# Issue order from estimated engine clocks, score bursts of three, and one shared set of PSUM banks in an attention and feed-forward kernel

## The chip, the cores and the metric

One core of a Trainium2 chip. The metric is the device time of one execution in microseconds (us); a *span* is the time from the first to the last instruction of the execution that was profiled. The kernel before takes 388.7 us (median of 3 runs, 388.52 to 390.5). The experiments ran in three batches, each on another chip (6, 8 and 13 in the record), and each batch timed the kernel before again, so a ratio compares runs of one batch. All runs told of here were in the fast state. The engines are called PE (TensorE), ACT (ScalarE), DVE (VectorE), POOL (GpSimd) and SP (SyncE, which issues most transfers).

## The reference

Attention with normalised queries and keys over 8 batches of 12 heads, 448 positions, 64 wide; then a feed-forward part over all 3584 positions.

```python
q_n, k_n = rmsnorm(q, g_q), rmsnorm(k, g_k)           # over the 64
scores = scale * np.matmul(q_n, k_n.transpose(0, 1, 3, 2))
attn = softmax(scores)                                # over the keys
x = np.matmul(attn, v)            # -> (3584, 768), heads side by side
a, b = x @ w1, x @ w2             # (768, 1024) each
h = a * b @ w3                    # (1024, 1024)
out = h @ w_out                   # (1024, 768), float32
```

Both kernels multiply w3 by w_out once (the matmuls called wps), so that the last two products are one.

## The kernel before

The kernel treats four heads at a time, 24 such sets. A set is 7 *score units*; a unit is 8 matmuls (sc) into two banks of PSUM, the memory that matmuls write to, and one exponential on ACT (P, or Pr for the last unit of a set). Three *pv* sets follow: one sums the exponentials (its logarithm and exponential, r, come from ACT), two give x (DVE multiplies by r into xT). Three sets of heads make a batch; then come its 8 pairs of pa (x times w1, copied to a_sb) and pb (x times w2, multiplied by a_sb into abT) and its po groups (copied to o_sb and stored). While PE has no work at the start, it runs matmuls whose results nobody reads (warm). All this is laid out in slots of two score units by tables:

```python
    sc_psum = ctx.enter_context(tc.tile_pool(name="sc_ps", bufs=2, space=PSUM))   # 2 x 2 banks
    mm_psum = ctx.enter_context(tc.tile_pool(name="mm_ps", bufs=4, space=PSUM))   # 4 x 1 bank
    ffn_pool = ctx.enter_context(tc.tile_pool(name="ffn", bufs=2))     # a_sb
    out_pool = ctx.enter_context(tc.tile_pool(name="outp", bufs=2))    # o_sb
    # ... tables: which slot has which part of the preparation, how many wps ...

    def qk_exp(n):
        # ...
        sc = sc_psum.tile([NP, 2, 512], FP, tag="sc", name="sc")
        for c0 in range(0, NP, 32):
            # ...
            for u in range(2):
                nc.tensor.matmul(
                    out=sc[c0 : c0 + 32, u, 0:S],
                    lhsT=qkT[u * D : (u + 1) * D, pr, 1, k0 : k0 + 32],
                    rhs=qkT[u * D : (u + 1) * D, pr, 0, 0:S],
                    start=True, stop=True, tile_position=(u * D, c0),
                )
        # ...
        nc.scalar.activation(out=dst, in_=sc[:, :, 0:S], func=AF.Exp)

    # a_sb is always copied by ACT, o_sb always by DVE:
        nc.scalar.copy(out=a_sb, in_=ps[:, 0:S])
        nc.vector.tensor_copy(out=o_sb[:, nh * NH : (nh + 1) * NH], in_=ps[:, 0:NH])

        for t in range(max(todo) + 1):
            # ... loads of this slot
            for n in range(2 * t, min(2 * t + 2, NQ * NU)):
                qk_exp(n)
            # ...
            for i, kind in todo.get(t, []):
                pv_set(i, kind)
            # ... weight loads, wps, or so many pa/pb/po from the list
            # ... preparation (square, reduce, scale, transpose) of later heads
```

Of the kernel before, what the change touches and what calls it, by code (L numbers as in the profile page):

```python
# [18 lines left out]
def kernel(  # L19
# [31 lines left out]

    const = ctx.enter_context(tc.tile_pool(name="const", bufs=1))
# [6 lines left out]
    ffn_pool = ctx.enter_context(tc.tile_pool(name="ffn", bufs=2))  # L59
    out_pool = ctx.enter_context(tc.tile_pool(name="outp", bufs=2))  # L60
    sc_psum = ctx.enter_context(tc.tile_pool(name="sc_ps", bufs=2, space=PSUM))
    mm_psum = ctx.enter_context(tc.tile_pool(name="mm_ps", bufs=4, space=PSUM))
# [3 lines left out]
    N_PE_T = 5  # L66
    N_SQ_ACT = 24
    W34_EV = 'DA'
    W34_NARROW = False
    WARM = (16, 2, 11, 3, 5, 0)  # L70
    LAG = 8
    UNITS = 3.0
    V_COST = 0.4
    V_AHEAD = 2
    MOVE = 2
    LOADS_0 = ['w0', 'w3', 'w1', 'o0', 'w2']
    LOADS_1 = ['w4', 'v0', 'w7', 'w6', 'w5', 'v1', 'o1', 'v2']
    GATE = ('q', 2)
    QK1_AT = 0
    SHIFT = [0, -1, -1, -1, -3, -3, -3]  # L80
    PREP_1 = {'sq0': -3, 'red0': -6, 'sq1': -6, 'red1': -3, 'alpha': -8, 'sc0': -3, 't0': -2, 'sc1': -2, 't1': 0}
    PREP = {'load': -7, 'sq0': -5, 'red0': -5, 'sq1': -4, 'red1': -4, 'alpha': -3, 'sc0': -3, 't0': -1, 'sc1': -2, 't1': -1}
    W34_SLOTS = {1: 2, 2: 1, 3: 2, 4: 3, 5: 1, 6: 1, 7: 3, 8: 1, 9: 1, 10: 2, 11: 2, 12: 3, 13: 2}
# [18 lines left out]

    qk_bufs = [
# [6 lines left out]
    halves = ((0, REST, J, 0, SPLIT), (REST, NP, NF, SPLIT, S))  # L110

# [6 lines left out]
    def load_qk(i, split=1, k_eng=None):  # L118
        b, m = divmod(i, NQB)
        s = st[i]  # L120
        s["q"], s["k"] = qk_bufs[i % 3]
        n = HQ // split
        for h0 in range(0, HQ, n):
            for t_sb, src, eng in (
                (s["q"], q, nc.sync),
                (s["k"], k, k_eng or nc.sync),
            ):
                for p0, p1, nj, t0, t1 in halves:
                    eng.dma_start(  # L129
                        out=t_sb[p0:p1, h0 : h0 + n, 0:nj, :].rearrange(  # L130
                            "p h j d -> p h (j d)"
                        ),
                        in_=src[b, HQ * m + h0 : HQ * m + h0 + n, t0:t1].rearrange(
                            "h (p j) d -> p h (j d)", j=nj
                        ),
                    )
# [57 lines left out]
    def prep_sq(i, pr, on_act=False):  # L194
        s = st[i]
        if pr == 0:
            s["ssq"] = prep_pool.tile([NP, 2, HQ, J], FP, tag="ssq", name="ssq")
        sq = prep_pool.tile([NP, 2, 2, J, D], FP, tag="sq", name="sq")
        s["sq", pr] = sq
        hs = slice(2 * pr, 2 * pr + 2)  # L200
        for t, src in enumerate((s["q"], s["k"])):
            if on_act:
                nc.scalar.activation(out=sq[:, t], in_=src[:, hs], func=AF.Square)  # L203
            else:
                nc.gpsimd.tensor_tensor(
                    out=sq[:, t], in0=src[:, hs], in1=src[:, hs], op=MULT
                )

    def prep_red(i, pr):
        s = st[i]  # L210
        hs = slice(2 * pr, 2 * pr + 2)
        sq = s.pop(("sq", pr))
        for t in ((0, 1), (1, 2)) if i == 0 else ((0, 2),):
            nc.vector.tensor_reduce(  # L214
                out=s["ssq"][:, slice(*t), hs, :], in_=sq[:, slice(*t)], axis=AX, op=ADD
            )

    def prep_alpha(i, h0=0, h1=HQ):
        s = st[i]
        if h0 == 0:  # L220
            s["lnv"] = prep_pool.tile([NP, 2, HQ, J], FP, tag="lnv", name="lnv")
            s["alpha"] = prep_pool.tile([NP, 2, HQ, J], FP, tag="alpha", name="alpha")
        lnv = s["lnv"][:, :, h0:h1]
        nc.scalar.activation(out=lnv, in_=s["ssq"][:, :, h0:h1], func=AF.Ln, bias=eps_t)
        nc.scalar.activation(  # L225
            out=s["alpha"][:, :, h0:h1], in_=lnv, func=AF.Exp, scale=-0.5
        )

    def prep_scale(i, pr, pe=False):
        s = st[i]  # L230
        hs = slice(2 * pr, 2 * pr + 2)
        if pr == 0:
            s["qkT"] = qkT_pool.tile([128, 2, 2, J * NP], BF, tag="qkT", name="qkT")
        alpha = s["alpha"]
        qtmp = prep_pool.tile([NP, J, 2, D], BF, tag="qtmp", name="qtmp")
        nc.vector.tensor_tensor(  # L236
            out=qtmp.transpose([0, 2, 1, 3]),
            in0=s["q"][:, hs],
            in1=alpha[:, 0, hs].unsqueeze(3).broadcast_to([NP, 2, J, D]),
            op=MULT,  # L240
        )
        qks = prep_pool.tile([NP, 2, J, 2, D], BF, tag="qks", name="qks")
        nc.vector.tensor_tensor(
            out=qks[:, 0],
            in0=qtmp,
            in1=g_b.unsqueeze(1).unsqueeze(1).broadcast_to([NP, J, 2, D]),
            op=MULT,
        )
        nc.vector.tensor_tensor(  # L249
            out=qks[:, 1].transpose([0, 2, 1, 3]),  # L250
            in0=s["k"][:, hs],
            in1=alpha[:, 1, hs].unsqueeze(3).broadcast_to([NP, 2, J, D]),
            op=MULT,
        )
        if pe:
            s["qks", pr] = qks
        else:
            issued.add(("t", i, pr))
            nc.sync.dma_start_transpose(
                out=s["qkT"][:, pr].rearrange("d t (j p) -> d (t j) p", p=NP),  # L260
                in_=qks.rearrange("p t j h d -> p (t j h d)"),
            )

    def prep_pe_transpose(i, pr):
        s = st[i]
        issued.add(("t", i, pr))
        qks = s.pop(("qks", pr))
        ps = mm_psum.tile([128, 2, S], BF, tag="mm", name="qkT_ps")
        for t in range(2):
            for j in range(J):  # L270
                n = NP if j < NF else REST
                nc.tensor.transpose(  # L272
                    ps[:, t, j * NP : j * NP + n], qks[0:n, t, j], ident[0:n, 0:n]
                )
        nc.vector.tensor_copy(out=s["qkT"][:, pr, :, 0:S], in_=ps)  # L275
# [4 lines left out]
    def qk_exp(n):  # L280
        i, g = divmod(n, NU)
        s = st[i]
        if g == 0:
# [3 lines left out]
        sc = sc_psum.tile([NP, 2, 512], FP, tag="sc", name="sc")  # L287
# [21 lines left out]
        nc.scalar.activation(out=dst, in_=sc[:, :, 0:S], func=AF.Exp)  # L309


    def pv_set(i, kind):
        s = st[i]
        b, m = divmod(i, NQB)
        ps = mm_psum.tile([128, S], FP, tag="mm", name="pv")
        for j in range(J):
            for h in range(HQ):
# [11 lines left out]
                )  # L329
        if kind == 0:  # L330
            s["r"] = att_pool.tile([128, S], FP, tag="r", name="r")
            nc.scalar.activation(out=s["r"], in_=ps, func=AF.Ln)
            nc.scalar.activation(out=s["r"], in_=s["r"], func=AF.Exp, scale=-1.0)
            return
        if b not in xT:
            xT[b] = x_pool.tile([128, CM, S], BF, tag="xT", name="xT")
        nc.vector.tensor_tensor(  # L337
            out=xT[b][:, 2 * m + kind - 1, :], in0=ps, in1=s["r"], op=MULT
        )
        if kind == 2:  # L340
# [4 lines left out]

    def w34_evac(dst, src, kind):
        if W34_EV[kind] == "A":
            nc.scalar.copy(out=dst, in_=src)
        else:
            nc.vector.tensor_copy(out=dst, in_=src)  # L350
# [11 lines left out]

    def w3_transpose(fc):
        assert ("w3", fc) in issued
        ps = mm_psum.tile([128, CF, 128], BF, tag="mm", name="w3T_ps")
# [4 lines left out]
        w34_evac(w3T[:, :, fc * 128 : (fc + 1) * 128], ps, 0)  # L370

    def w34_unit(fc, nh):
        assert ("o", nh) in issued
        ps = mm_psum.tile([128, 512], FP, tag="mm", name="wps")
        for gc in range(CF):
            lhsT = w3T[:, gc, fc * 128 : (fc + 1) * 128]
            rhs = w_outs[:, gc, nh * NH : (nh + 1) * NH]
            if W34_NARROW:
                narrow(ps, NH, lhsT, rhs, gc == 0, gc == CF - 1)
            else:  # L380
                nc.tensor.matmul(  # L381
                    out=ps[:, 0:NH], lhsT=lhsT, rhs=rhs,
                    start=(gc == 0), stop=(gc == CF - 1),
                )
        w34_evac(w34s[:, fc, nh * NH : (nh + 1) * NH], ps[:, 0:NH], 1)
# [3 lines left out]
    def ffn1_a(b, fi):  # L389
        ps = mm_psum.tile([128, 512], FP, tag="mm", name="pa")  # L390
# [6 lines left out]
        nc.scalar.copy(out=a_sb, in_=ps[:, 0:S])  # L397
        a_tiles[b, fi] = a_sb

    def ffn1_b(b, fi):  # L400
# [3 lines left out]
        ps = mm_psum.tile([128, 512], FP, tag="mm", name="pb")  # L404
        for c in range(CM):
# [4 lines left out]
        nc.vector.tensor_tensor(  # L410
            out=abT[bp][:, fi, odd * S : (odd + 1) * S],
            in0=ps[:, 0:S],
            in1=a_tiles.pop((b, fi)),
            op=MULT,
# [4 lines left out]
    def ffn2(bp, t, nh):  # L419
# [3 lines left out]
        ps = mm_psum.tile([128, 512], FP, tag="mm", name="po")  # L423
# [238 lines left out]
```

## Time and profile before

The numbers come from the trace: starts of PE's groups of matmuls, and the distance from each to the next.

| part of the span, us | before |
|---|---|
| up to the first pa | 71.3 |
| work after it, at PE's pace | 291.0 |
| entering and leaving score bursts after it (69 x 0.228) | 15.7 |
| all other loss after it | 4.9 |
| last matmul to the end | 4.3 |
| span | 387.2 |

"At PE's pace" means 47.25 ns for a matmul of 448 columns in a 32-column strip (four run side by side), 40.6 ns for one of 384, and 23.6 ns for a score matmul (eight side by side). In the lines of a profile, 128*128, 128*32 and 64*32 are PE's *tiling modes*: the rows and columns of its array that one matmul takes. The table is a difference of starts, not of busy time: the ends of matmuls are modelled, so a late start can hide inside a busy PE. The lines behind it are shown in the prediction below.

### The profile page before, as it was taken

How to read it: one execution, taken by the hardware profiler on the slowest of the kernel's cores; microseconds unless marked ns; L12 is line 12 of the kernel's file. 1: busy time of each engine (PE TensorE's matmuls, PEld its weight loads, DVE VectorE, ACT ScalarE, POOL GpSimd, SP SyncE). 2: the span in 40 equal slices, each digit the busy share in tenths (PEclk: the TensorE clock that was granted, in tenths of full speed). 3: DMA queues.
4: the chain of work that ended last, by engine and by line, in shares of the span. 5: the costliest groups of instructions: out<-in, count | busy, mean ns of one | idle time of the engine just before them, and what ended most of it. 6: DMA issues, size and time to landing. Idle time of an engine off the chain costs nothing.

```text
span 387.2 us, 17022 instructions
## 1 busy us (share of the span) xinstructions
PE 372.7 (96%) x7669; PEld 192.1 (50%) x7670; DVE 242.5 (63%) x398; ACT 265.7 (69%) x443; POOL 75.5 (19%) x131
## 2 busy tenths in 40 slices
PE   7869999999999998999999999999999999999995
PEld 2335545444544454444545455445544554556563
DVE  5877855557758665776678568587676684234232
ACT  3578897778678883888697866786788856730210
POOL 2526546322022202202202202220222000000000
PEclk9969999999999999999999999999999999999998
DMA  6999999787989839849978879868898564004005
GB/s 176 220 239 231 234 232 169 114 108 160 153 163 178 161 68 232 192 68 154 228 139 157 124 171 197 149 146 158 173 175 152 65 153 86 3 3 125 2 19 149
DMA packets 92972, 56.42 MB, mean 146 GB/s; under 512 B 56932, under 2 KB 86884, under 8 KB 92900
## 3 DMA queue, kind: packets, MB, share of 16 engines
q1 hardware_dynamic: 70208, 42.35, 50.8%
q0 software_dynamic: 21952, 12.33, 23.9%
q8 instruction: 60, 0.98, 1.1%
q10 hardware_dynamic: 740, 0.66, 0.7%
q14 instruction: 12, 0.10, 0.1%
HBM read 46.66 MB, written 11.01 MB: 149 GB/s over the span
## 4 chain that ended last, share of the span: by engine, by line
PE 79%; DMA 10%; DVE 4%; ACT 3%; SPq 2%; issue 1%; POOL 1%; DVEq 0%; ACTq 0%; POOLq 0%
PE pa L354 17%; PE pb L354 17%; PE po L354 15%; PE pv L322 13%; PE sc L297 9%; PE wps L381 6%; DMA out_dram<-o_sb 5%; DMA w_outs<-in_moe_w_out_dram 4%; PE qkT_ps L272 1%; ACT P L309 1%; DVE o_sb L430 1%; DVE ssq L214 1%; SPq L129 1%; DMA q_sb<-in_q_dram 1%; PE w3T_ps L367 1%
## 5 line engine op out<-in xcount | busy, mean ns | idle before, releaser
L309 ACT ACTIVATE P<-sc 128x896 bf16<-128x896 f32 x144 | 125.1, 913 | 28.9 <-PE sc L297 28.8
L354 PE MATMUL pa<-xT,w1s 128*32 128x448 bf16 x1536 | 83.9, 353 | 1.1 <-DVE xT L337 1.1
L354 PE MATMUL pb<-xT,w2s 128*32 128x448 bf16 x1536 | 83.8, 352 | 0.0
L152 POOL DMA_DIRECT2D v_sb<-in_v_dram x72 | 43.7, 620 | 198.1 <-PE pv L322 174.5
L354 PE MATMUL po<-w34s,abT 128*32 128x384 bf16 x1792 | 77.5, 326 | 1.7 <-DVE o_sb L430 1.7
L410 DVE TENSOR_TENSOR abT<-pb,a_sb 128x448 bf16<-128x448 f32 x64 | 39.8, 622 | 60.1 <-PE pb L354 45.6
L214 DVE TENSOR_REDUCE ssq<-sq 128x16 f32<-128x1024 f32 (+1 forms) x50 | 58.2, 1168 | 12.2 <-ACT sq L203 12.2
L397 ACT CAST a_sb<-pa 128x448 bf16<-128x448 f32 x64 | 33.9, 530 | 43.4 <-PE pa L354 43.3
L354 PEld LDWEIGHTS <-abT 128*32 128x32 bf16 x1792 | 48.1, 97 | 28.5 <-issue 2.2
L354 PEld LDWEIGHTS <-w1s 128*32 128x32 bf16 x1536 | 40.4, 97 | 34.8 <-issue 5.4
L354 PEld LDWEIGHTS <-w2s 128*32 128x32 bf16 x1536 | 41.4, 97 | 31.3
L430 DVE COPY o_sb<-po 128x384 f32<-128x384 f32 x56 | 30.4, 555 | 39.3 <-PE po L354 20.9
L297 PE MATMUL sc<-qkT 64*32 64x448 bf16 x1344 | 48.9, 357 | 0.2 <-DVE qkT L275 0.2
L236 DVE TENSOR_TENSOR qtmp<-q_sb,alpha 128x512 bf16<-128x512 f32 x48 | 32.9, 684 | 12.8 <-ACT alpha L225 10.9
L322 PE MATMUL pv<-P,v_sb 128*32 128x448 bf16 x576 | 36.0, 356 | 0.0
L337 DVE TENSOR_TENSOR xT<-pv,r 128x448 bf16<-128x448 f32 x48 | 29.6, 616 | 5.2 <-PE pv L322 3.4
L249 DVE TENSOR_TENSOR qks<-k_sb,alpha 128x512 bf16<-128x512 f32 x48 | 32.9, 684 | 0.0
L203 ACT ACTIVATE sq<-q_sb 128x512 f32<-128x512 f32 x48 | 30.2, 630 | 0.0
L203 ACT ACTIVATE sq<-k_sb 128x512 f32<-128x512 f32 x48 | 29.9, 623 | 0.0
L322 PEld LDWEIGHTS <-v_sb 128*32 128x32 bf16 x768 | 16.2, 95 | 24.0 <-issue 15.5
L297 PEld LDWEIGHTS <-qkT 64*32 64x32 bf16 x1344 | 12.2, 89 | 28.8 <-issue 27.4
L381 PE MATMUL wps<-w_outs,w3T 128*128 128x384 bf16 x128 | 24.7, 345 | 1.1 <-DMA w_outs<-in_moe_w_out_dram 1.1
(46 smaller groups left out, 243.3 us busy)
## 6 DMA issues: line engine op xcount, KB each, us to landing
out_dram<-o_sb SPq DMA_DIRECT2D x54, 192.0 KB, 3.3
q_sb<-in_q_dram SPq DMA_DIRECT2D x23, 256.0 KB, 3.8
k_sb<-in_k_dram SPq DMA_DIRECT2D x23, 256.0 KB, 4.7
q_sb<-in_q_dram SPq DMA_DIRECT2D x23, 192.0 KB, 4.4
k_sb<-in_k_dram SPq DMA_DIRECT2D x23, 192.0 KB, 5.4
v_sb<-in_v_dram POOLq DMA_DIRECT2D x24, 96.0 KB, 4.2
w3s<-in_moe_w_dram POOLq DMA_DIRECT2D x8, 256.0 KB, 9.6
w_outs<-in_moe_w_out_dram POOLq DMA_DIRECT2D x4, 384.0 KB, 10.7
```

The costliest lines, as they stand in the source:

```text
L152: nc.gpsimd.dma_start(out=dst.rearrange("p h j d -> p h (j d)"), in_=part.rearrange("p h j d -> p h (j d)"),)
L203: nc.scalar.activation(out=sq[:, t], in_=src[:, hs], func=AF.Square)
L214: nc.vector.tensor_reduce(out=s["ssq"][:, slice(*t), hs, :], in_=sq[:, slice(*t)], axis=AX, op=ADD)
L236: nc.vector.tensor_tensor(out=qtmp.transpose([0, 2, 1, 3]), in0=s["q"][:, hs], in1=alpha[:, 0, hs].unsqueeze(3).broadcast_to([NP, 2, J, D] ...
L297: nc.tensor.matmul(out=sc[c0 : c0 + 32, u, 0:S], lhsT=qkT[u * D : (u + 1) * D, pr, 1, k0 : k0 + 32], rhs=qkT[u * D : (u + 1) * D, pr, 0, 0:S],
L309: nc.scalar.activation(out=dst, in_=sc[:, :, 0:S], func=AF.Exp)
L322: nc.tensor.matmul(out=ps[h * HALF : (h + 1) * HALF, :], lhsT=w, rhs=s["P"][:, h, j, :] if j < NF else s["Pr"][:, h % 2, :], start=(j == 0 ...
L354: nc.tensor.matmul(out=ps[32 * h : 32 * h + 32, 0:n], lhsT=lhsT[:, 32 * h : 32 * h + 32], rhs=rhs, start=start, stop=stop, tile_position=( ...
L381: nc.tensor.matmul(out=ps[:, 0:NH], lhsT=lhsT, rhs=rhs, start=(gc == 0), stop=(gc == CF - 1),)
L397: nc.scalar.copy(out=a_sb, in_=ps[:, 0:S])
L410: nc.vector.tensor_tensor(out=abT[bp][:, fi, odd * S : (odd + 1) * S], in0=ps[:, 0:S], in1=a_tiles.pop((b, fi)), op=MULT,)
L430: nc.vector.tensor_copy(out=o_sb[:, nh * NH : (nh + 1) * NH], in_=ps[:, 0:NH])
```

## The change

Its intent is to let a model of each engine's clock, kept while the program is built, decide what is issued next, instead of tables. At the start the model also picks PE's next work. After that PE's order is still laid out by score unit (a pv set stands KIND units behind the last burst of its heads, and pa, pb and po are spread over what is left); the model then chooses the banks, the engine of each copy, and what ACT and DVE do in between. Scores come three units at a time. Any of the eight PSUM banks may serve any stage, the one that is estimated to be free first. A copy out of PSUM goes to the engine that is estimated to end it first. Weight loads are all queued at the start, behind a *gate*: a small copy on POOL that waits for a first transfer of queries. The queries of the first batch lie on 112 partitions, four rows each, so that one transfer brings them.

```diff
-    ffn_pool = ctx.enter_context(tc.tile_pool(name="ffn", bufs=2))
-    out_pool = ctx.enter_context(tc.tile_pool(name="outp", bufs=2))
-    sc_psum = ctx.enter_context(tc.tile_pool(name="sc_ps", bufs=2, space=PSUM))
-    mm_psum = ctx.enter_context(tc.tile_pool(name="mm_ps", bufs=4, space=PSUM))
+    G = 3
+    KIND = (3, 4, 6)
+    ffn_pool = ctx.enter_context(tc.tile_pool(name="ffn", bufs=F_BUFS))      # 3
+    out_pool = ctx.enter_context(tc.tile_pool(name="outp", bufs=O_BUFS))     # 3
+    ps_pool = ctx.enter_context(tc.tile_pool(name="ps", bufs=1, space=PSUM))
+    banks = ps_pool.tile([128, 8, 512], FP, name="banks_ps")
+    clk = {"PE": 0.0, "ACT": 0.0, "DVE": 0.0}
+    free = [0.0] * 8
+    def take(n):
+        z = min(range(9 - n), key=lambda a: (max(free[a : a + n]), a % n, a))
+        # ...
+    def evac(z, ready, engs, costs, fn):
+        ends = [max(clk[e], ready) + c + (BIAS if k else 0) for k, (e, c) in enumerate(zip(engs, costs))]
+        k = ends.index(min(ends))
+        # ... other work of ACT and DVE that fits before is issued first
+        fn(e)
# ... prep_red, prep_alpha and prep_scale in smaller pieces; queries on 112 partitions
-        nc.scalar.copy(out=a_sb, in_=ps[:, 0:S])
+        at = copy_out(z, a_sb, ps[:, 0:S], A_EV, S)             # A_EV = O_EV = "AD"
-        nc.vector.tensor_copy(out=o_sb[:, nh * NH : (nh + 1) * NH], in_=ps[:, 0:NH])
+        copy_out(z, o_sb[:, nh * NH : (nh + 1) * NH], ps[:, 0:NH], O_EV, NH)
# ...
+            if (t - t0) % G == 0 and t < NQ * NU:
+                flush_exps()
+                for n in range(t, min(t + G, NQ * NU)):
+                    qk_exp(n)
# ... the tables and their loop removed
```

## The prediction

> **What bounds the kernel now.** I read the table of busy times first, then the order of PE's work in time, the waits of PE, and the stretches. On the page:
>
> ```profile
> span 387.2 us, 17022 instructions
> PE 372.7 (96%) x7669; PEld 192.1 (50%) x7670; DVE 242.5 (63%) x398; ACT 265.7 (69%) x443; POOL 75.5 (19%) x131
> L309 ACT ACTIVATE P<-sc 128x896 bf16<-128x896 f32 x144 | 125.1, 913 | 28.9 <-PE sc L297 28.8
> L354 PE MATMUL pa<-xT,w1s 128*32 128x448 bf16 x1536 | 83.9, 353 | 1.1 <-DVE xT L337 1.1
> ```
>
> PE is busy 96% of the span and no other engine 70%. But 96% cannot be taken as distance from the limit, because the ends of matmuls are modelled. What tells is the distance between starts, in the timeline of PE alone (start, duration, what, count), taken from the steady middle:
>
> ```profile
> 161.98 0.36 PE L322 MATMUL pv<-Pr,v_sb 128*32 128x448 bf16 x4
> 162.17 1.31 PE L354 MATMUL pa<-xT,w1s 128*32 128x448 bf16 x24
> 163.30 1.31 PE L354 MATMUL pb<-xT,w2s 128*32 128x448 bf16 x24
> 164.54 0.57 PE L297 MATMUL sc<-qkT 64*32 64x448 bf16 x16
> 165.04 1.32 PE L354 MATMUL pa<-xT,w1s 128*32 128x448 bf16 x24
> 166.19 1.31 PE L354 MATMUL pb<-xT,w2s 128*32 128x448 bf16 x24
> 167.32 1.31 PE L354 MATMUL pa<-xT,w1s 128*32 128x448 bf16 x24
> 168.56 0.57 PE L297 MATMUL sc<-qkT 64*32 64x448 bf16 x16
> ```
>
> From pa at 162.17 to pb at 163.30 are 1.135 us: 24 matmuls of 448 columns, four side by side, so 0.189 us for each four. That is PE's streaming pace. From pb at 163.30 to sc at 164.54 are 1.24 us: 0.104 us lost before the scores. The 16 score matmuls go eight at a time (2 row halves, 4 column strips), so two units should take 2 x 0.189 = 0.378 us, but the next group starts 0.502 us later: 0.124 lost behind them. **One burst of scores costs 0.228 us beyond its work**, however long it is. There are 1344/16 = 84 bursts: 19.2 us, 5% of the span.
>
> Add up the work at this pace: pa and pb 128 x 1.135, po 56 x 1.30 (32 matmuls of 384), pv 72 x 0.757, sc 168 x 0.189, the w3 x w_out product 16 x 1.30, its transposes 8 x 0.455, the q/k transposes 10 x 0.44: about 333 us of 387. The missing 54 us: 19 at the bursts, about 5 waits in the middle, 4.3 from the last matmul to the end (last copy and store), and the rest in the first 71 us, before the first pa (71.3 us). There it is arrival and waits:
>
> ```profile
> 17.81 0.83 PE L367 MATMUL w3T_ps<-ident,w3s 128*128 128x128 bf16 x12
> 21.16 1.07 PE L272 MATMUL qkT_ps<-ident,qks 128*128 128x128 bf16 x8 [2.52 <-DVE qks L243]
> 22.67 1.02 PE L381 MATMUL wps<-w_outs,w3T 128*128 128x384 bf16 x4
> 24.76 1.44 PE L381 MATMUL wps<-w_outs,w3T 128*128 128x384 bf16 x4 [1.07 <-DMA w_outs<-in_moe_w_out_dram]
> ```
>
> ```profile
> 20.00:30.00 10.00, 7.64 (x63) 3.57 (x64) 7.97 (x12) 7.43 (x11) 3.07 (x6) 0.66 1.21 240
> 73.00:340.00 267.00, 264.20 (x5964) 134.04 (x5960) 176.93 (x282) 205.69 (x340) 41.16 (x68) 1.00 0.77 144
> ```
>
> These stretches give busy us of PE, PEld, DVE, ACT, POOL, then granted clock, DMA share and GB/s. Between 20 and 30 us PE waited for q/k preparation and for half of w_out, and was granted 0.66 of its clock, with DMA share over 1. Later the clock is 1.00, ACT is busy 77%, DVE 66%. The waits of PE in the middle are few:
>
> ```profile
> PE po L354 <- DVE o_sb L430: 1.7, 2, 1.4
> PE pa L354 <- DVE xT L337: 1.1, 2, 0.5
> ```
>
> **What the Trainium skill says.** "TensorEngine Tiling (Array Packing)", Key Properties: changing the tiling mode, not just the tile, drains TensorE. The trace agrees: every entry to and exit from 64*32 among 128*32 groups costs 0.104 and 0.124 us, while pa to pb (same mode) costs nothing. "TensorE: Matmul & The Clock Gate", "What's actually happening": PE falls to half clock after an idle window of about 3.4 us and recovers after as long a busy one. The trace agrees roughly: after the two waits above, the stretch 24.7 to 28.9 us had a clock of 0.50. "Perfetto Trace Analysis", Identifying the Most-Contended Engine: matmul busy share is no measure of distance from the roofline; here 96% busy hid the 19 us of switches. "PSUM — Partial Sum Buffer", Specifications: eight banks a partition; a score unit takes two, so a burst of 3 holds six.
>
> **The change, part by part.** I compared the instruction orders of the two programs. Matmuls are the same save 45 warm-up ones for 37.
> - *Bursts.* 56 bursts of 24 matmuls in place of 84 of 16. 28 x 0.228 = **6.4 us** off PE's own path: 1.4 before the first pa (9 bursts for 15), 5.0 after (47 for 69).
> - *Where the first pa stands.* Work ahead of it: before 42.1 us + 15 bursts (3.4) + 9 changes between full and strip mode (0.106 each in the trace, 1.0) = 46.4; after 40.7 + 9 bursts (2.1) + 5 changes (0.5) = 43.3. So 3.1 us less, 1.4 of it merely moved behind (3 score units and one pv set).
> - *Loads.* All weight loads are issued at the start, behind a first q transfer (it landed at 4.2 us) and not a later one (gate opened at 7.6), half of w_out ahead of w3. In the trace a w3 piece takes about 1.65 us in the stream and each w_out transfer about 3.5, so the first w3 piece lands at 18 to 21 us (estimate) in place of 14.2, but then the product never waits for w_out. The loads of heads 4 to 11 also go at once. The 1.07 us wait and about 2 us of half clock may go; the later start of w3 work gives some back. I take 1.5 us gain, so the first pa at 71.3 - 3.1 - 1.5 = **66.7 us**.
> - *Copies out of PSUM.* Given at build time to whichever engine is estimated to be free first. ACT gets 42 of the 56 o_sb copies (0.48 us, from the w34s copy of the same shape) and gives up 11 of 64 a_sb (0.53) and 14 of 16 w34s. In the middle stretch ACT gains about 35 x 0.48 - 8 x 0.53 = 12.6 us: 218 of some 262, or 83%. DVE loses about as much there. Neither is then the bound.
> - *Buffers.* Three o_sb for two removes the wait that held po (1.4 us longest, then PE at once on scores); a po or pb now stands between the last pv of a batch and its pa, which covers the 0.5 us waits for xT. Of 5.0 us lost after the first pa in the old kernel I keep 1 and allow 2 for new waits.
> - *112 partitions.* The first queries come in one transfer of 4 rows each and not two; the squares, reductions and scalings keep their column counts and so their time. Worth a fraction of a microsecond in the start.
> - *Split reductions and logs* add 46 DVE instructions and a few on ACT, hidden.
>
> Sum: first pa 66.7; after it work 292.2 + 47 x 0.228 = 302.9, plus 3 for waits = 305.9; tail 4.3: span 376.9. The old timed run is 1.5 us above its span (388.7 to 387.2): **378.5 us**, 2.6% faster.
>
> **Rivals.** (a) *PSUM becomes the wait.* Six banks for scores leave two. Three exponentials at 0.82 us pitch need 2.5 us, in which PE runs two groups of 1.135 us that DVE must evacuate (0.62 each). For it: two banks only, ACT at 83%, strict orders fixed by estimates. Against: the estimated durations agree with the trace's (1.135 a group), and a period of three units is about 5.6 us. If each burst loses 0.1 to 0.2 us, the gain falls by 5 to 9 us: 384 to 387. (b) *DVE bounds the head.* Its work before the first abT: 24 reductions of 0.63, 10 scalings of 1.79 (three instructions), q/k copies 6, w34s 14 x 0.55, w3T 5 x 0.68, xT 3.7, memsets 3: 57 us of the 60 after its start. Before, it was 48. For it: that sum. If DVE holds PE, the first pa stays near 70 and the time is about 382. (c) *Loads bound the head*: DMA share is over 1 until 60 us in any case, and w1/w2 landed by 65. With them earlier I expect them by 60; else again about 382. (d) *Everything fits*: clock at full from the start, no waits behind the head: first pa 64, no waits: 374.
>
> **Range and chances.** (d) sets the low end, (a) with (b) in part the high end: 373 to 385. Faster by over 2% means below 380.9, 2.4 above my figure, which (b) or (c) alone would eat. I give 0.63 to faster, 0.34 to within 2%, and 0.03 to slower, since 6.4 us of removed switches stand against any new wait.
>
> **What would show it.** Right: sc in groups of 24 that take 3 x 0.189 + 0.124 to the next start; first pa at 65 to 69 us; PE's waits in the middle under 3 us; ACT about 83% there; clock near 1.0 after 20 us. Wrong: PE waiting at sc or pv for ACT's P or r (rival a), PE waiting for DVE's qks or qkT before 65 us (b), PE waiting for w3s or w1s DMAs (c), or a burst cost that grows with its length.

## The result

The changed kernel takes 379.35 us (median of 4 runs, 377.37 to 379.94) beside 389.6 us for the kernel before in the same rounds. A ratio here is the mean time of one kernel's fast runs over that of the other's of the same rounds, so it is not quite the ratio of the medians: 0.9728, interval 0.9678 to 0.9779. Predicted were 378.5 us, in 373 to 385.

In the changed kernel every PSUM tile is called banks_ps, so one goes by lines: L457 are the scores, L523 pa, pb and po, L487 pv, L551 wps, L539 the w3 transposes, L425 the q/k transposes; L203 is a copy on ACT, L205 one on DVE. From the page of the changed kernel:

```profile
span 377.4 us, 17123 instructions
PE 364.8 (97%) x7677; PEld 197.7 (52%) x7678; DVE 239.9 (64%) x425; ACT 280.3 (74%) x472; POOL 76.6 (20%) x133
```

PE in order of time (start, duration, what), in the steady middle:

```profile
78.20 1.31 PE L523 MATMUL banks_ps<-xT,w1s 128*32 128x448 bf16 x24
79.44 0.76 PE L457 MATMUL banks_ps<-qkT 64*32 64x448 bf16 x24
80.13 0.75 PE L487 MATMUL banks_ps<-P,v_sb 128*32 128x448 bf16 x12
```

The 24 matmuls of pa need 1.135 us and sc starts after 1.24: 0.104 lost, as before. From sc at 79.44 to pv at 80.13 are 0.69 us, and three units need 3 x 0.189 = 0.567: 0.125 lost, as before. A burst of three costs what a burst of two did.

Two stretches, and PE's two longest waits outside the start (total us, times, longest):

```profile
20.00:30.00 10.00, 8.87 (x117) 5.08 (x115) 8.77 (x19) 7.71 (x12) 4.13 (x8) 1.00 1.19 234
73.00:340.00 267.00, 264.63 (x6101) 142.59 (x6092) 175.95 (x301) 217.83 (x362) 41.21 (x68) 1.00 0.78 145
```

```profile
PE banks_ps L523 <- ACT a_sb L203: 1.8, 2, 1.6
PE banks_ps L457 <- DVE abT L589: 0.3, 1, 0.3
```

The clock between 20 and 30 us is 1.00 where it was 0.66. The half clock has not gone, it has moved: the traces have it from 23.2 to 30.0 us before, and from 11.5 to 15.0 us now, while PE runs warm-up matmuls and the first score burst. ACT is busy 217.8 of 267 us, 82%, where it was 77%. The waits for o_sb and for xT are gone, but a new one stands there: PE waits for an a_sb copy. The timeline around it shows why (the bracket gives the idle time before, and what ended it):

```profile
234.12 0.36 PE L487 MATMUL banks_ps<-Pr,ones 128*32 128x448 bf16 x4
...
235.02 0.63 ACT L335 ACTIVATE sq<-q_sb 128x512 f32<-128x512 f32 x1 [2.95 <-DMA q_sb<-in_q_dram]
235.56 0.51 ACT L203 CAST a_sb<-banks_ps 128x448 bf16<-128x448 f32 x1
...
236.12 1.32 PE L523 MATMUL banks_ps<-xT,w2s 128*32 128x448 bf16 x24 [1.64 <-ACT a_sb L203]
```

ACT stood idle for 2.95 us at the head of its queue, at a square whose q had not landed. The a_sb copy that would have freed a bank was behind it.

| part of the span, us | before | changed |
|---|---|---|
| up to the first pa | 71.3 | 66.0 |
| work after it, at PE's pace | 291.0 | 292.3 |
| score bursts after it, x 0.228 | 15.7 (69) | 10.7 (47) |
| all other loss after it | 4.9 | 4.4 |
| last matmul to the end | 4.3 | 4.0 |
| span | 387.2 | 377.4 |

Of the 9.8 us, 5.0 are bursts after the first pa. The start gives 5.3: 1.3 is work that merely moved behind the first pa, 1.4 are six bursts fewer (6 x 0.228), and the remaining 2.6 are fewer waits and mode changes and a faster clock.

Where the starts of PE's groups lie further apart than the pace and the bursts explain, one can place the other loss of 4.4 us: 2.2 are two waits for an a_sb copy behind a late load (at 236 us and, smaller, at 154), 1.4 are four stalls inside or right behind a score burst (for one of them the trace names abT, 0.3 us), and the rest is spread thin.

### The profile page after: what moved, and what is told of

The parts are those of the page before. It is cut to its first block, busy times and chain, and to the rows that moved or that the text cites. A ratio compares the mean times of both kernels' runs of the same rounds, so it can differ in the third digit from the quotient of the medians.

```text
span 377.4 us, 17123 instructions
## 1 busy us (share of the span) xinstructions
PE 364.8 (97%) x7677; PEld 197.7 (52%) x7678; DVE 239.9 (64%) x425; ACT 280.3 (74%) x472; POOL 76.6 (20%) x133
## 3 DMA queue, kind: packets, MB, share of 16 engines
q0 software_dynamic: 22016, 12.33, 24.4%
## 4 chain that ended last, share of the span: by engine, by line
PE 85%; DMA 8%; ACT 3%; SPq 1%; issue 1%; DVE 0%; ACTq 0%; DVEq 0%
PE banks_ps L523 54%; PE banks_ps L487 15%; PE banks_ps L457 9%; DMA k_sb<-in_k_dram 5%; PE banks_ps L551 5%; DMA q_sb<-in_q_dram 3%; ACT P L471 1%; PE banks_ps L425 1%; PE banks_ps L539 1%; ACT a_sb L203 1%; SPq L629 1%; SPq L254 1%; ACT sq L335 0%; ACT o_sb L203 0%; DVE o_sb L205 0%
## 5 line engine op out<-in xcount | busy, mean ns | idle before, releaser
L471 ACT ACTIVATE P<-banks_ps 128x896 bf16<-128x896 f32 x144 | 124.2, 922 | 14.0 <-PE banks_ps L457 13.7
L523 PE MATMUL banks_ps<-xT,w2s 128*32 128x448 bf16 x1536 | 83.8, 352 | 1.8 <-ACT a_sb L203 1.8
L523 PE MATMUL banks_ps<-xT,w1s 128*32 128x448 bf16 x1536 | 83.9, 353 | 0.0
L523 PE MATMUL banks_ps<-w34s,abT 128*32 128x384 bf16 x1792 | 77.8, 326 | 0.0
L344 DVE TENSOR_REDUCE ssq<-sq 128x8 f32<-128x512 f32 (+1 forms) x96 | 63.5, 679 | 13.9 <-ACT sq L335 13.3
L589 DVE TENSOR_TENSOR abT<-banks_ps,a_sb 128x448 bf16<-128x448 f32 x64 | 39.8, 622 | 41.8 <-PE banks_ps L523 41.5
L523 PEld LDWEIGHTS <-abT 128*32 128x32 bf16 x1792 | 47.8, 97 | 26.5 <-DVE abT L589 0.3
L523 PEld LDWEIGHTS <-w2s 128*32 128x32 bf16 x1536 | 41.5, 97 | 33.4 <-issue 2.7
L523 PEld LDWEIGHTS <-w1s 128*32 128x32 bf16 x1536 | 40.8, 97 | 31.9 <-issue 2.2
L203 ACT CAST a_sb<-banks_ps 128x448 bf16<-128x448 f32 x53 | 28.1, 530 | 25.9 <-PE banks_ps L523 25.1
L457 PE MATMUL banks_ps<-qkT 64*32 64x448 bf16 x1344 | 44.4, 357 | 0.7 <-DVE abT L589 0.3
L376 DVE TENSOR_TENSOR qtmp<-q_sb,alpha 128x512 bf16<-128x512 f32 (+1 forms) x48 | 33.0, 687 | 11.8 <-ACT alpha L360 10.3
L203 ACT COPY o_sb<-banks_ps 128x384 f32<-128x384 f32 x42 | 20.1, 478 | 23.1 <-PE banks_ps L523 23.0
L487 PE MATMUL banks_ps<-P,v_sb 128*32 128x448 bf16 x576 | 35.8, 354 | 0.0
L335 ACT ACTIVATE sq<-q_sb 128x512 f32<-128x512 f32 (+1 forms) x48 | 30.0, 625 | 5.6 <-DMA q_sb<-in_q_dram 5.6
L487 PEld LDWEIGHTS <-v_sb 128*32 128x32 bf16 x768 | 18.9, 96 | 18.7 <-issue 6.9
L457 PEld LDWEIGHTS <-qkT 64*32 64x32 bf16 x1344 | 15.1, 90 | 25.9 <-issue 21.0
```

What stands on the lines that cost most here:

```text
L203: nc.scalar.copy(out=out, in_=in_)
L335: nc.scalar.activation(out=s["sq", pr][0:n, t], in_=(s["q"], s["k"])[t][0:n, 2 * pr : 2 * pr + 2], func=AF.Square,)
L344: nc.vector.tensor_reduce(out=s["ssq"][0:n, t, 2 * pr : 2 * pr + 2, :], in_=s["sq", pr][0:n, t], axis=AX, op=ADD,)
L376: nc.vector.tensor_tensor(out=s["qtmp"][0:n].transpose([0, 2, 1, 3]), in0=s["q"][0:n, hs], in1=alpha[0:n, 0, hs].unsqueeze(3).broadcast_to ...
L457: nc.tensor.matmul(out=sc[c0 : c0 + 32, u, 0:S], lhsT=qkT[u * D : (u + 1) * D, pr, 1, k0 : k0 + 32], rhs=qkT[u * D : (u + 1) * D, pr, 0, 0:S],
L471: lambda: nc.scalar.activation(out=dst, in_=sc[:, :, 0:S], func=AF.Exp),
```

## The experiments

In each table of numbers, "other loss" is the fourth row of the table above. Kernels called "changed" start from the changed kernel, those called "old" from the kernel before.

### Does a burst have a fixed cost? Bursts of one and of two

Edit, for one unit (for two: G = 2, KIND = (2, 3, 4); for two with later pv: KIND = (4, 5, 6)):

```diff
-    G = 3
-    KIND = (3, 4, 6)
+    G = 1
+    KIND = (1, 2, 3)
```

> Bursts of one score unit (162 bursts). If the cost is per burst and does not depend on its length: 106 more bursts x 0.228 = 24 us more, about 403.5 us. If long bursts cost more each, or PSUM waits behind long bursts give part back, the step from 3 to 1 is under 18 us. Rival of ordering: within 3 us of 379.4.

> The changed kernel with bursts of 2 score units and not 3 (84 bursts for 56, two of them of one unit), everything else the same program that orders itself. Theory that the bursts carry most of the gain after the first pa: 28 x 0.228 us = 6.4 us more, about 385.7 us, and the trace shows the same 0.10 + 0.125 us at each burst. Rival, that the ordering by estimated clocks carries the gain and the bursts do not matter: within 1.5 us of the changed kernel's 379.4.

> Bursts of two units once more, with the pv sets one burst later behind the last score unit of their heads. The first run with bursts of 2 gave 395.9 us, of which 6.4 us were expected; its trace had some 10 us of PE waits at pv for ACT's P and Pr. Theory that those came from pv standing only one burst of two units behind the scores, and not from the burst length: waits at pv under 2 us, 385 to 387.5. Rival, that the ordering is only good for bursts of 3: 391 or more.

| kernel | bursts | us, median | ratio to before | span | first pa | bursts after it | other loss |
|---|---|---|---|---|---|---|---|
| changed | 56 | 379.35 | 0.9728 | 377.4 | 66.0 | 10.7 | 4.4 |
| bursts of 1 | 162 | 404.25 | 1.0418 | 401.8 | 65.2 | 33.3 | 6.0 |
| bursts of 2 | 84 | 395.9 | 1.0183 | 395.6 | 66.0 | 16.6 | 15.8 |
| bursts of 2, later pv | 84 | 392.75 | 1.0114 | 391.0 | 66.5 | 16.6 | 10.7 |

Bursts of one: 24.4 us more span for 106 more bursts, 0.230 us each; 24 were expected. The span also holds 1.6 us more other loss and a first pa 0.8 us earlier, so the timeline is the better witness. It shows the same loss at a single unit:

```profile
152.97 0.38 PE L457 MATMUL banks_ps<-qkT 64*32 64x448 bf16 x8
153.28 0.75 PE L487 MATMUL banks_ps<-P,v_sb 128*32 128x448 bf16 x12
```

0.31 us for 0.189 of work, 0.12 lost behind it. Over all 146 bursts of this run after the first pa, the median loss is 0.104 us before a burst and 0.124 behind it, as with 69 bursts of two in the old kernel and 47 of three in the changed one (0.104 and 0.125). The cost is per burst, whatever its length.

Bursts of two came out 10 us worse than the 6.4 that the bursts cost. Those 10 us are waits, and some 1.6 of them half clock after the longest one. There PE stood 2.71 us at pv until 173.75 us, while ACT took two squares, waited 0.83 us for DVE's sums and only then took Pr; from 174.3 to 177.7 us the clock was 0.50. Moving pv one burst later took 5 of them away, as part of the theory said, but 10.7 us of other loss remained, and PE now waited at the scores for banks:

```profile
PE banks_ps L457 <- ACT P L471: 3.5, 5, 1.1
PE banks_ps L457 <- ACT a_sb L203: 2.9, 7, 0.6
```

At 392.75 us the run is on the side of the rival: the order as it stands is good for bursts of three (and has little loss with one), and is slower than the old kernel with two. Why the order for two lets ACT fall behind I have not followed further; that stays open. So the step from two to three in this kernel is worth more than its bursts, but only 6.4 us of it are shown to be the bursts' own.

### Is the burst enough? Bursts of three in the old kernel

```diff
-    p_pool = ... name="P", bufs=2        sc_psum ... bufs=2        mm_psum ... bufs=4
+    p_pool = ... name="P", bufs=3        sc_psum ... bufs=3        mm_psum ... bufs=2
-            todo.setdefault(at + 1 + kind, []).append((i, kind))
+            todo.setdefault(at + 2 + kind, []).append((i, kind))
-            for n in range(2 * t, min(2 * t + 2, NQ * NU)):
-                qk_exp(n)
+            if t % 3:
+                for n in range(6 * (t // 3) + 3 * (t % 3) - 3, min(6 * (t // 3) + 3 * (t % 3), NQ * NU)):
+                    qk_exp(n)
```

> The kernel before with bursts of 3 alone: three pairs of banks for scores and two single banks for all else, the two bursts of every six units in two of three slots, pv sets one slot later, three P buffers, copies on fixed engines as before. The switches save 28 x 0.228 = 6.4 us. Theory that bursts of 3 need the shared banks and the copies on the free engine: a_sb copies on ACT stand behind three exponentials while only two banks are left, PE waits for them, and most or all of the 6.4 us is given back: 386 to 400. Rival, that the burst alone gives the gain: 382 to 384.

433.25 us (ratio 1.1154), worse than I had expected, and for another reason: PE's waits for a_sb are 1.0 us in all. The bursts after the first pa cost 10.5 us as they should, but the other loss is 40.8 us, and the first pa came at 86.1, with 20.5 us at half clock before it. A stretch of the timeline:

```profile
101.58 2.52 ACT L309 ACTIVATE P<-sc 128x896 bf16<-128x896 f32 x3
...
103.97 0.56 ACT L332 ACTIVATE r<-pv 128x448 f32<-128x448 f32 x1
...
104.58 0.75 PE L354 MATMUL pa<-xT,w1s 128*32 128x448 bf16 x12 [1.84 <-ACT r L332]
```

pv holds one of the two single banks until ACT has taken its logarithm (r), which stands behind three exponentials (2.52 us). The next pa starts when r has been taken. The other bank was free from 103.45, when DVE had made abT of the pb in it, but this kernel's pool did not give it out: pa waited for the one that pv had. The edit has three parts besides the burst (six and two banks, pv later, a third P buffer), so it shows that bursts of three in this division and order lose, not which of the two is at fault. The next two runs split that.

### Shared banks, and copies on the free engine

Banks divided again, six and two, in the changed kernel:

```diff
     def take(n):
-        z = min(range(9 - n), key=lambda a: (max(free[a : a + n]), a % n, a))
+        own = (0, 2, 4) if n == 2 else (6, 7)
+        z = min(own, key=lambda a: (max(free[a : a + n]), a % n, a))
# ... the same in the second choice, and three pairs where a burst asks for banks
```

> The changed kernel with its banks divided again: three pairs for scores, two single banks for all else; the order is made anew under that limit, copies still go to the estimated free engine. In the kernel before, bursts of 3 under this division cost 433 us, with 41 us of PE waits after the first pa. Theory that sharing the banks is what makes bursts of 3 possible: PE waits for copies out of the two banks, 10 us or more, 390 or above. Rival, that the order and the choice of engine suffice: under 384.

Copies on fixed engines, banks shared:

```diff
-    A_EV = "AD"
-    O_EV = "AD"
+    A_EV = "A"
+    O_EV = "D"
```

> The changed kernel with a_sb always copied by ACT and o_sb always by DVE, as before; banks shared, bursts of 3, head unchanged. Theory that the choice matters because three exponentials hold ACT for 2.5 us while a_sb waits: waits of PE for ACT's a_sb rise by 3 to 8 us, 382 to 387. Rival, that shared banks absorb it: within 1.5 us of the changed kernel.

| kernel | us, median | ratio to before | span | first pa | other loss |
|---|---|---|---|---|---|
| changed | 379.35 | 0.9728 | 377.4 | 66.0 | 4.4 |
| six and two banks | 413.79 | 1.0637 | 409.9 | 77.3 | 27.8 |
| copies on fixed engines | 384.76 | 0.9869 | 383.8 | 65.5 | 11.2 |

With six and two banks, PE waits at pv (L488 there) for copies on both engines:

```profile
PE banks_ps L488 <- DVE abT L590: 8.0, 10, 0.8
PE banks_ps L488 <- DVE o_sb L206: 4.4, 6, 0.7
PE banks_ps L488 <- DVE a_sb L206: 3.5, 4, 1.3
PE banks_ps L488 <- ACT a_sb L204: 3.2, 3, 1.4
```

So the sharing is what makes bursts of three pay here: with six and two banks, the same program that orders itself and chooses engines loses 23.4 us more after the first pa, and its first pa comes 11.3 us later (up to 3.4 of that is clock: 6.8 us at half clock, from 19.1 to 25.9). About 4 us of its loss stand behind late q loads, as in the next run. Its settings, such as KIND, are those made for shared banks; others were not tried. With fixed copies:

```profile
PE banks_ps L487 <- ACT a_sb L203: 2.8, 2, 1.6
PE banks_ps L523 <- ACT a_sb L203: 1.8, 1, 1.8
```

6.8 us more loss, in the expected range of 3 to 8, but not for the expected reason, so the number was met partly by luck. The timeline around one of these waits:

```profile
280.47 0.63 ACT L335 ACTIVATE sq<-q_sb 128x512 f32<-128x512 f32 x1 [3.13 <-DMA q_sb<-in_q_dram]
281.00 0.51 ACT L203 CAST a_sb<-banks_ps 128x448 bf16<-128x448 f32 x1
...
281.57 0.75 PE L487 MATMUL banks_ps<-P,ones 128*32 128x448 bf16 x12 [1.56 <-ACT a_sb L203]
```

It is not three exponentials that stand before the copy, but a square that waited 3.13 us for its q. By the distances between starts, 7.3 of the 11.2 us of loss stand at six such places, against 2.2 of 4.4 us at two in the changed kernel, with the same order of PE in both; waits of po for abT make another 1.8. ACT's waits for q and k loads are 15.7 us here and 8.8 there, probably because ACT, which has no o_sb copies, comes to its squares sooner. So fixed copies cost 5.4 us of time as long as the loads are late. What the choice of engine is worth with loads in time was not run.

### What the third buffers are worth

```diff
-    ffn_pool = ctx.enter_context(tc.tile_pool(name="ffn", bufs=2))
-    out_pool = ctx.enter_context(tc.tile_pool(name="outp", bufs=2))
+    ffn_pool = ctx.enter_context(tc.tile_pool(name="ffn", bufs=3))
+    out_pool = ctx.enter_context(tc.tile_pool(name="outp", bufs=3))
```

> The kernel before with three buffers and not two for o_sb and a_sb, nothing else. In its trace PE lost 1.6 and 0.5 us at po, where DVE's o_sb copy waited for the store of an older o_sb. Theory: those waits go, 2 us or 0.5% off, about 386.5. Rival: the bank behind stays the limit and nothing changes: within 0.7 us.

This is the old kernel, with nothing else changed: 384.94 us, ratio 0.9914 (0.9883 to 0.9945), so 0.9% faster, more than the 0.5% that I expected. Other loss after the first pa fell from 4.9 to 1.0 us. I had counted only PE's waits for o_sb. The waits for xT went too, and DVE's waits in the two kernels show the link. DVE in the old kernel, then with three buffers:

```profile
DVE o_sb L430 <- DMA out_dram<-o_sb: 16.1, 7, 4.4
```

```profile
DVE o_sb L430 <- DMA out_dram<-o_sb: 1.3, 1, 1.3
```

DVE stood 16.1 us, up to 4.4 at a time, at an o_sb copy that waited for a store, with everything else of DVE behind it. With three buffers 1.3 us of this are left. The way to PE can be followed: after such a wait of 3.06 us (until 110.39) DVE's ssq was late, so ACT waited 1.01 us for it; from there on ACT's logarithm and a_sb and DVE's abT come about 1.1 us later, measured from PE's pa, than with three buffers, and so does the xT for which PE waited 0.55 us at 121.29. The two buffers were not tried apart; no wait of ACT for an a_sb buffer stands in the old kernel's trace.

### The start: the gate and the 112 partitions

```diff
-    GATE = ("q", 0)
+    GATE = ("q", 2)
```

> The changed kernel with the weight loads held until the transfer of the second half of the first queries, as the gate of the kernel before did; the order of all engines is the same. The gate then opens some 3 us later (7.3 for 4.0 us), and the w3 and w_out pieces land up to 3 us later, so the first w3 transposes move from 19.6 to about 22, and the first pa from 66.0 to 67 to 69: 380.5 to 382.5. Rival, that the head is bound by PE's work and preparation from 25 us on and the loads are hidden: first pa unchanged within 0.5 us.

379.77 us, ratio 0.9751; first pa at 65.6. The rival holds. The first w_out transfer was issued at 8.4 us instead of 4.1, but the first w3 piece landed at 20.2 instead of 19.2: the DMA engines were busy either way (their share between 10 and 20 us is 1.20 here and 1.18 in the changed kernel).

Queries in two transfers on 128 partitions again (the output of the first batch then in pieces of 64 rows, as before):

```diff
-    parts_of = lambda b, t: ((0, NP0, J, 0, S),) if b == 0 and t == 0 else halves
-    rows_of = lambda i, t: NP0 if i < NQB and t == 0 else NP
+    parts_of = lambda b, t: halves
+    rows_of = lambda i, t: NP
# ... two more transfers at the start, zeros in the tails of the query buffers
```

> The changed kernel with the first queries in two transfers on 128 partitions, as before, and not on 112. The first transposes need both halves, so they start up to 0.5 us later; but PE is filled with warm-up matmuls until the first w3 piece lands at 19 us, so theory: first pa and time unchanged within 1 us of 379.4. Rival: the shorter start carries part of the gain: 1.5 us or more slower.

380.1 us, ratio 0.9792 (0.9759 to 0.9824) against 0.9728 (0.9678 to 0.9779): the intervals overlap, so the time does not settle it. In the trace the first pa came at 67.3, 1.3 us later, a little more than the 1 us that the theory allowed; the end of PE's work was the same (373.4 in both), because less was lost later. At most a microsecond of the gain lies here.

One more fact bears on the start. The old kernel with three buffers has the same instructions in the same order on PE, ACT, DVE and POOL as the old kernel, and had its first pa at 69.5 and not 71.3. The stretch 24.7 to 28.9 us in the old kernel (the granted clock is the third number from the end):

```profile
24.70:28.90 4.20, 4.14 (x32) 1.95 (x32) 2.63 (x3) 2.67 (x5) 1.40 (x3) 0.50 1.23 235
```

The same stretch in the old kernel with three buffers:

```profile
24.70:28.90 4.20, 4.20 (x45) 2.27 (x43) 3.16 (x5) 3.16 (x6) 1.58 (x4) 0.88 1.26 228
```

In one execution PE was at half clock for 6.8 us (23.2 to 30.0), in the other for 3.4 (22.3 to 25.7), a difference worth at most 1.7 us of PE's time. So up to 1.8 us of the 5.3 at the start, and of the 2.6 that are neither work nor bursts, is chance of the execution that was profiled. All runs of the changed kernel that left its instructions before the first pa alone and its queries on 112 partitions had it between 65.0 and 66.0.

### Is the new wait for a_sb a matter of late loads?

First, squares placed later in ACT's queue:

```diff
-            push_prep(n, LAND.get("q%d" % n, clk["PE"] + 6.0))
+            push_prep(n, LAND.get("q%d" % n, clk["PE"] + 9.0))
```

> The changed kernel with the squares of the next heads taken to be ready 9 us after their loads' issue and not 6, so that ACT's queue has them later. In its trace PE waited 1.8 us at 235 us and 0.35 at 153 for an a_sb copy that stood in ACT's queue behind a square which waited for a q load (ACT idle 2.95 us for that load). Theory: this wait goes, PE's waits for ACT fall from 1.8 us to under 0.5, 377 to 378 us. Rival: the square is then late for its transpose and scores wait for it: 380 or more.

379.05 us, ratio 0.976: nothing gained, other loss 4.7. The wait for ACT was gone, and another had come:

```profile
172.26 0.61 DVE L205 CAST a_sb<-banks_ps 128x448 bf16<-128x448 f32 x1
172.79 1.27 DVE L344 TENSOR_REDUCE ssq<-sq 128x8 f32<-128x512 f32 x2
173.98 0.62 DVE L589 TENSOR_TENSOR abT<-banks_ps,a_sb 128x448 bf16<-128x448 f32 x1
174.65 0.67 PE L523 MATMUL banks_ps<-w34s,abT 128*32 128x384 bf16 x12 [1.49 <-DVE abT L589]
```

With the squares moved, this a_sb copy went to DVE and the reductions stood between it and abT; po needed that abT. The theory was right about the wait for ACT and wrong about the time; the rival, late scores, did not come either.

Then the loads themselves earlier, with the squares where they were:

```diff
-    LOAD_AT = -17
+    LOAD_AT = -23
# ... and 9.0 as above; the order of PE, ACT, DVE and GpSimd is then that of the changed kernel
```

> The changed kernel with the q and k loads of later heads issued up to 6 score units earlier; the instruction order of PE, ACT, DVE and GpSimd is identical, only the queue of SyncE differs. Theory: ACT's waits for q and k loads (5.6 and 3.2 us in the changed kernel) go, and with them PE's 1.8 us wait for a_sb behind them: 376.5 to 378. Rival: the earlier loads or their waits for free buffers delay DMA transposes in the same queue: 379.5 or more.

376.73 us (6 runs, 376.08 to 377.11), ratio 0.9675 (0.9643 to 0.9708): the fastest of all. Its six runs lie below all four of the changed kernel (377.37 to 379.94), though the intervals of the two ratios overlap, so the half per cent between them is likely rather than settled. The run with the late gate is a closer match: same batch and chip, the same order of all engines. Its four runs (378.5 to 380.38) lie above all six, and the intervals do not overlap (0.9709 to 0.9793). Other loss is 2.2 us and the PE stretch that carries the kernel is full:

```profile
73.00:340.00 267.00, 266.44 (x6156) 143.61 (x6144) 175.68 (x300) 218.88 (x363) 41.13 (x68) 1.00 0.79 142
```

ACT's waits in it, of those that end with a load:

```profile
ACT sq L335 <- DMA k_sb<-in_k_dram: 1.7, 2, 0.9
```

This is the only wait of ACT for a load that is left (8.8 us before). The traces have the same order of PE, ACT, DVE and POOL as the changed kernel, so only SP's queue differed, and this shows that late loads caused the a_sb wait. The four stalls at score bursts are still there (1.4 of the 2.2 us).

Last, two w3 pieces ahead of w_out, on top of this version:

```diff
-    LOADS = ["o0", "w0", "w1", "w2", ...
+    LOADS = ["w0", "w1", "o0", "w2", ...
# ... and the times at which the model expects them
```

> The version with early loads (376.7 us), with two w3 pieces loaded ahead of the first half of w_out. In the changed kernel PE ran 16 us of warm-up matmuls until the first w3 piece landed at 19.2 us. Theory: two w3 transposes move into that filler, the first product starts at 20.5 to 22 and not at 22.7, the first pa comes 1 to 2 us earlier: 375 to 376. Rival: w_out, landing later, becomes the wait, or preparation on DVE holds PE: 376.5 to 378.

377.85 us, ratio 0.9733: not faster. The first product started at 19.8 us and not at 22.7, but PE then waited for w_out (0.8 us) and q/k preparation, and the first pa came at 66.0. The rival holds: work pulled forward at the start is waited away before 30 us.

## Why the prediction was right

**The pace and the cost of a burst** were right, and carry the result: 0.104 and 0.125 us at each burst of three, 0.230 us each over 106 bursts, 5.0 us after the first pa and 1.4 before it, as worked out.

**The first pa** was put at 66.7 us and came at 66.0. The work that moves (1.4 predicted, 1.3 measured) and the bursts (1.4) were right. What is left, mode changes, waits and clock, was put at 0.4 + 1.5 = 1.9 us and measured 2.6, and its reason was partly wrong: I gave it to the earlier gate, and the run with a late gate has the same first pa. Up to 1.8 of the 2.6 is chance of the profiled execution, so that this term came out near is partly luck. The prediction's reading of the clock was loose, too: it puts the half clock after both of PE's waits, but the trace has it from 23.2 us, after the wait of 2.52 us and before the one of 1.07 ended.

**Copies.** ACT at 83% was predicted and 82% measured. That neither engine is the bound was right. That DVE would lose about as much as ACT gains, some 12 us, was not: DVE was busy 176.0 us of the stretch and 176.9 before.

**Waits after the first pa** are the term that was mis-sized. The prediction said: "Of 5.0 us lost after the first pa in the old kernel I keep 1 and allow 2 for new waits." The first half is what the old kernel with three buffers showed, 1.0 us. The new waits are 3.4 us and not 2: 2.2 because a square waiting for a late q load stood before an a_sb copy in ACT's queue, which I did not see, and 1.4 in the stalls at score bursts. So nearly all that the third buffers gave was given back, and the early loads won 2.2 us of it again. The waits for xT, which I meant to cover with another order, go with the third buffers alone.

**The rivals.** (a) PSUM as the wait is small in the changed kernel: the 2.2 us at a_sb copies and the 1.4 at bursts after the first pa, and 0.9 us at 25 us behind an exponential; no pv waited for P or r. It is what happens without sharing (27.8 us of loss). (b) DVE was busy 8.8 of 10 us between 20 and 30, as the sum of its work said, but the trace names no wait of PE for q/k preparation or its copies between 25 us and the first pa. (c) The loads did not bound the first pa within the 1 us by which the late gate moved them. (d) Not everything fitted: 379.35 us and a first pa at 66.0, for 374 and 64; with early loads it is 376.73 and 65.0.

Sum: 66.0 against 66.7, 307.4 against 305.9 from the first pa to the last matmul, 4.0 against 4.3: a span of 377.4 against 376.9. The span is so near because a first pa 0.7 us too late and waits 1.4 us too small partly cancel. The last 0.4 us of time is the distance from span to timed run. (The prediction's sum gives 378.4, not 378.5. It took the distance as 1.5 us from the median of the old runs; the profiled one took 389.01 us, 1.8 above its span.)

## What to carry to other kernels

Measure PE by the distance between starts of its groups; a mode change that costs 0.23 us shows there, and grouping by mode pays only if PSUM banks and copies can follow, which here took banks shared by all stages. Copies on whichever engine is free saved 5.4 us as long as loads were late. ACT stood idle for 2.95 us at a square with a copy behind it, so a copy that frees a bank must not stand behind anything that waits for a transfer: issue the transfer earlier (some 0.5% here) rather than move the waiting instruction, which only moved the wait. Before rebuilding a schedule, try the cheap thing alone: a third buffer gave a third of the whole gain.

## What the Trainium skill lacked or had wrong

- "TensorEngine Tiling (Array Packing)" says that a mode change drains PE, but not what it costs: 0.104 us into 64*32 and 0.124 to 0.125 us back to 128*32, whatever the length between them (medians over bursts of one, two and three units).
- "PSUM — Partial Sum Buffer" gives eight banks and the advice to evacuate promptly, but nothing on dividing them among stages: with six and two banks in place of eight shared PE lost 23.4 us more after the first pa (about 4 of it behind late loads), and the first pa came 11.3 us later.
- No page that I read gives a size for how a wait for a transfer in one engine's queue reaches PE: 2.95 us of ACT at a late load became 1.64 us of PE, and with DVE's waits for stores down from 16.1 to 1.3 us PE's other loss fell by 3.9 us.
